# An fp32 attention + two-MoE kernel on one Trainium2 core: the second MoE's first product by seven block products instead of eight

## The chip, the cores and the metric

One core of one Trainium2 chip. The metric is device time in microseconds of one execution, the median of several runs. Engines: PE (TensorE), DVE (VectorE), ACT (ScalarE), POOL (GpSimd), SP (SyncE, which here issues most DMAs).

## What is computed

Attention with windowed masks gives x (2304 tokens x 512); a first MoE with a tanh gate gives x again; the second MoE, cut from the reference, is

```python
def _moe2_ref(x, w_in, w_out, g_ln):       # x 2304x512, w_in 512x1024, w_out 1024x512
    h = x @ w_in
    e = np.exp(h - np.max(h, axis=-1, keepdims=True))
    sm = e / (np.sum(e, axis=-1, keepdims=True) + 1e-09)
    solu = h * sm
    mu = np.mean(solu, axis=-1, keepdims=True)
    var = np.mean((solu - mu) ** 2, axis=-1, keepdims=True)
    ln = (solu - mu) / np.sqrt(var + 1e-06) * g_ln
    return ln @ w_out
```

All weights of the two MoEs are float64 at the entry.

## The kernel before

Every large product is made of three passes of float32r matmuls: each operand is split into a high part and a low part, and high x high, high x low and low x high are summed in PSUM. So one product of a 128-token tile by a 128 x 512 block of weights is three matmuls of 512 columns.

*First MoE.* Six groups of 384 tokens, 16 slices of the hidden width each; a step s does `mm1(s)` (12 matmuls into one of two banks h, L348), then `mm2(s - 5)` (12 matmuls, L375). Between them ACT and DVE make tanh (L356), the difference (L359, which frees the h bank) and its high and low parts (L362, L365). `NS` is the number of steps, 96; the last group is steps 80 to 95.

*Weights.* Each 128 x 512 block of a weight is loaded as raw int64 words (`w_load`, L90 to L95) and turned to float32 high and low parts by `w_step` (L102): ACT makes a "top" half (L111), DVE ORs it to the rest (L123), ACT makes the high part (L117), DVE the low part (L98). For the second MoE these 16 blocks are made during steps 81 to 100, one per step, into the buffers of the first MoE's `w_in`, each of which is free once the last group has used it.

*Second MoE.* 18 tiles of 128 tokens. The tokens come back from DRAM in pairs of tiles (`load_y`, L434) and are split by `split_y`: one cast on DVE (L440), one subtraction on POOL (L441), 1024 wide. Per tile: `mm3` makes h, 24 matmuls of 512 columns into two banks (L523); `softmax` (L532 to L542) takes the maximum on DVE, Exp on ACT, the product h*e on DVE, the mean and the subtraction on DVE; `fac` squares on ACT (L548) and does seven operations of one column on POOL (L549 to L555); `trz` transposes z in eight matmuls into two banks `zt` (L566) and splits it with eight pairs of 128-column instructions that also multiply by g_ln (L574, L575); `mm4` is 24 matmuls against the second weight (L585); `store` scales and writes out (L592). The loop over tiles issues `trz(i)`, `store(i-1)`, `mm3(i+2)`, `fac(i+1)`, every other time `split_y` and `load_y`, then `mm4(i)` and `softmax(i+2)`.

The order of each engine's queue is the order in which the program issues (`manual_schedule`); a queue is worked off in order, so an instruction that waits holds all behind it. Pools set which buffers are reused, and with that most waits.

Of the kernel before, what the change touches and what calls it, by code (L numbers as in the profile page):

```python
# [20 lines left out]
NTOK = B * S  # L21
# [19 lines left out]
def tile_kernel(ctx: ExitStack, tc: tile.TileContext, qk, vw, cst, w_in, w_out, w_in2, w_out2, g_ln, out):  # L41
# [5 lines left out]
    wo_p = tc.alloc_tile_pool(name="wo", bufs=1, side="left")  # L47
# [3 lines left out]
    x_p = ctx.enter_context(tc.tile_pool(name="x", bufs=2, side="right"))  # L51
# [213 lines left out]
    def pv_pe(u, pool, tag):  # L265
# [3 lines left out]
        x = xt[g, hp] = x_p.tile([128, 2, G], F32R, tag=f"x{hp}", name=f"x{g}_{hp}")  # L269
# [122 lines left out]
    def plan():  # L392
# [3 lines left out]
        for u in range(u0, u1 + 2):  # L396
# [27 lines left out]
    w2i, w2o = [None] * (2 * KD), [None] * NF2  # L424
    wq2 = [(w2i, 2 * k + n, wi_p, w_in2[k, n], f"wi{2 * k + n}", f"w2i{2 * k + n}")
           for k in range(KD) for n in range(2)]
    wq2 += [(w2o, j, wi_p, w_out2[j], f"wi{2 * KD + j}", f"w2o{j}") for j in range(NF2)]

    yt, y_raw = {}, {}

    def load_y(j):
        if j < NTOK // YT:
            y_raw[j] = p2.tile([128, KD, YT], F32, tag="yr", name=f"yr{j}")
            nc.sync.dma_start(out=y_raw[j], in_=y_dr[:, :, j * YT:(j + 1) * YT])  # L434

    def split_y(j):
        if j < NTOK // YT:
# [12 lines left out]
    for s in range(NS + LAG):  # L450
        if s == NS - NF:
            assert not todo and not later and not (wq or wld or wa or wf or wh), (todo, later)
            a_ps.release()
            at_p.release()
            qs_p.release()
            cv_p = tc.alloc_tile_pool(name="cv2", bufs=2, side="left", reuse_waits="tile")
            new_tops()
            h2a = tc.alloc_tile_pool(name="h2a", bufs=1, space=PSUM, side="right", reuse_waits="tile")
            p2 = tc.alloc_tile_pool(name="p2", bufs=2, side="right", reuse_waits="tile")
            wq.extend(wq2)  # L460
            w_load()
            w_load()
        for half in range(2):
# [8 lines left out]
            if s < NF + LAG and done[0] < W0 + WA * (slot + 1) // WB or s > NS - NF and half == 0:  # L472
                w_step()
                done[0] += 1
            follow = [fn() for fn in todo.pop(slot, [])]
# [25 lines left out]
    while wq or wld or wa or wf or wh:  # L501
        w_step()
# [12 lines left out]
    def mm3(i):  # L515
        y = yt[i // 2]
        o = (i % 2) * TT
        ps = (h2a if i % 2 == 0 else h2b).tile([128, FF2], F32, tag="h2", name=f"h2_{i}")
        for n in range(2):
            q = 0  # L520
            for k in range(KD):
                for a, b in ((0, 0), (0, 1), (1, 0)):
                    nc.tensor.matmul(ps[:, n * 512:(n + 1) * 512], y[:, a, k, o:o + TT], w2i[2 * k + n][:, b],  # L523
                                     start=(q == 0), stop=(q == 3 * KD - 1))
                    q += 1
        st[i] = dict(h=ps)

    def softmax(i):

        d = st[i]  # L530
        ps = d["h"]
        sml = p3.tile([128, 8], F32, tag="sml", name=f"sml{i}", bufs=4)  # L532
        d["sml"] = sml
        nmax, ssum, usum, nmean = (sml[:, c:c + 1] for c in range(4))
        e = p3.tile([128, FF2], F32, tag="e", name=f"e{i}")
        u = p3.tile([128, FF2], F32, tag="u", name=f"u{i}")
        d["z"], d["junk"] = e, u
        nc.vector.tensor_reduce(out=nmax, in_=ps, axis=mybir.AxisListType.X, op=ALU.max, negate=True)
        nc.scalar.activation(out=e, in_=ps, func=AF.Exp, bias=nmax, accum_out=ssum)  # L539
        nc.vector.scalar_tensor_tensor(out=u, in0=ps, scalar=1.0, in1=e, op0=ALU.mult, op1=ALU.mult, accum_out=usum)  # L540
        nc.vector.tensor_scalar(out=nmean, in0=usum, scalar1=-1.0 / FF2, scalar2=None, op0=ALU.mult)
        nc.vector.tensor_scalar(out=e, in0=u, scalar1=nmean, scalar2=None, op0=ALU.add)  # L542

    def fac(i):
# [3 lines left out]
        nc.scalar.activation(out=d["junk"], in_=d["z"], func=AF.Square, accum_out=ssq)  # L548
# [8 lines left out]
    def trz(i):  # L557

        d = st[i]
        z = p3.tile([128, 2, NF2, TT], F32R, tag="z", name=f"z{i}")  # L560
        pp = []
        for n in range(2):
            ps = zo.tile([128, 512], F32, tag="zt", name=f"zt{i}_{n}").rearrange("p (j t) -> p j t", t=TT)
            for j in range(4):
                c = 4 * n + j
                nc.tensor.transpose(ps[:, j], d["z"][:, c * TT:(c + 1) * TT], ident)  # L566
            pp.append(ps)
        for n in range(2):
            g = gl_sb[:, 4 * n:4 * n + 4].unsqueeze(2).to_broadcast([128, 4, TT])
            zh, zl = z[:, 0, 4 * n:4 * n + 4], z[:, 1, 4 * n:4 * n + 4]  # L570
            for j in range(4):
                c = 4 * n + j
                gc = gl_sb[:, c:c + 1]
                nc.scalar.activation(out=z[:, 0, c], in_=pp[n][:, j], func=AF.Copy, scale=gc)  # L574
                nc.vector.scalar_tensor_tensor(out=z[:, 1, c], in0=pp[n][:, j], scalar=gc,  # L575
                                               in1=z[:, 0, c].bitcast(F32), op0=ALU.mult, op1=ALU.subtract)
        d["zt"] = z

    def mm4(i):
        z = st[i]["zt"]  # L580
# [111 lines left out]
```

## Time and profile before

| | |
|---|---|
| runs | 729.39, 727.55, 728.31 us; median 728.31 |
| span of the profiled execution | 726.3 us |
| PE busy | 708.8 us (98%), 4160 matmuls |
| DVE, ACT, POOL busy | 440.5, 386.9, 114.4 us |
| second MoE | from 504 us to the end |

The span runs from the first to the last instruction of one profiled execution; the runs' times contain what lies around it. In the page's 40 slices PE stands at 9 tenths from the fourth slice to the last but one, with the granted clock at 9 (90% or more) throughout. `x24` means 24 instructions; `out<-in` are the program's names without buffer numbers; a duration given as a mean is that of one instruction.

### The profile page before, as it was taken

To read this page: it belongs to the slowest core of one execution; us is meant where nothing else is said; L and a number is where in the kernel's file an instruction comes from. 1 tells how busy PE (TensorE), PEld (TensorE's weight loads), DVE (VectorE), ACT (ScalarE), POOL (GpSimd) and SP (SyncE) were. 2 spreads that over 40 slices of the span, in tenths; PEclk is the share of its full clock that TensorE was granted. 3 is DMA by queue.
4 is the path that set the end of the run, shared out by engine and by line. 5 is a ranking of instruction groups with operands and counts; after the bars stand their busy time and mean duration, and the time that the engine had idled before them with its cause. 6 is when DMAs were issued, how large, how long until landed. Compare 5 with 4: busy or idle time off the path is not lost.

```text
span 726.3 us, 11583 instructions
## 1 busy us (share of the span) xinstructions
PE 708.8 (98%) x4160; PEld 650.7 (90%) x4160; DVE 440.5 (61%) x1169; ACT 386.9 (53%) x1010; POOL 114.4 (16%) x190
## 2 busy tenths in 40 slices
PE   6888999999999999999999999999999999999997
PEld 5678999999999999999999999999888888888885
DVE  5987676476676667766666435554555454555452
ACT  5778776465555555555555334543354444444444
POOL 2212311011010111111110100101133221323110
PEclk9999999999999999999999999999999999999999
DMA  9985621132223211322230015543001110110001
GB/s 274 341 263 177 189 78 55 65 110 66 66 66 109 66 60 44 107 66 66 66 109 1 1 49 170 175 142 132 1 15 59 44 58 16 59 44 30 15 29 44
DMA packets 30313, 64.05 MB, mean 88 GB/s; under 512 B 2992, under 2 KB 16816, under 8 KB 30256
## 3 DMA queue, kind: packets, MB, share of 16 engines
q1 hardware_dynamic: 27088, 58.59, 25.4%
q10 hardware_dynamic: 3168, 4.72, 1.8%
q8 instruction: 33, 0.54, 0.3%
q14 instruction: 24, 0.20, 0.1%
HBM read 53.86 MB, written 9.44 MB: 87 GB/s over the span
## 4 chain that ended last, share of the span: by engine, by line
PE 92%; DVE 4%; DMA 1%; issue 1%; ACT 1%; POOL 0%; SPq 0%; ACTq 0%; POOLq 0%
PE y L375 28%; PE h L348 26%; PE po L585 14%; PE h L523 14%; PE zt L566 2%; PE pv L275 2%; PE tp L254 2%; PE qkp L219 2%; PE qkp L199 2%; DMA qkr<-in_qk_dram 1%; DVE p L204 1%; DVE wy_wi L123 1%; DVE wi L98 1%; DVE wi L134 0%; POOL p L247 0%
## 5 line engine op out<-in xcount | busy, mean ns | idle before, releaser
L348 PE MATMUL h<-x,wi 128*128 128x384 f32 x1152 | 220.0, 340 | 1.6 <-DVE t L359 1.6
L375 PE MATMUL y<-gs,wo 128*128 128x384 f32 x1152 | 217.4, 339 | 0.0
L375 PEld LDWEIGHTS y<-gs,wo 128*128 128x128 f32 x1152 | 199.8, 189 | 1.8
L348 PEld LDWEIGHTS h<-x,wi 128*128 128x128 f32 x1152 | 197.4, 189 | 3.2 <-DVE t L359 2.1
L247 POOL TENSOR_TENSOR p<-p,rs 96x512 f32<-96x512 f32 x47 | 57.2, 1217 | 350.4 <-DVE rs L245 323.5
L365 DVE TENSOR_TENSOR gs<-t,gs 128x384 fp32r<-128x384 f32 x96 | 77.4, 806 | 52.7 <-ACT gs L362 52.6
L523 PE MATMUL h<-w2i,yt 128*128 128x512 f32 x432 | 104.9, 397 | 0.0
L585 PE MATMUL po<-w2o,z 128*128 128x512 f32 x432 | 104.1, 396 | 0.1
L574 ACT ACTIVATE z<-zt,gl_sb 128x128 fp32r<-128x128 f32 x144 | 50.9, 366 | 96.6 <-PE zt L566 48.5
L585 PEld LDWEIGHTS po<-w2o,z 128*128 128x128 f32 x432 | 80.7, 188 | 20.4 <-ACT z L574 1.9
L523 PEld LDWEIGHTS h<-w2i,yt 128*128 128x128 f32 x432 | 79.7, 187 | 18.4
L359 DVE TENSOR_TENSOR t<-h,t 128x384 f32<-128x384 f32 x96 | 53.0, 552 | 69.8 <-ACT t L356 69.7
L575 DVE SCALAR_TENSOR_TENSOR z<-zt,gl_sb,z 128x128 fp32r<-128x128 f32 x144 | 48.9, 350 | 68.9 <-ACT z L574 68.9
L356 ACT ACTIVATE t<-h 128x384 f32<-128x384 f32 x96 | 46.8, 487 | 79.4 <-PE h L348 76.4
L239 ACT ACTIVATE p<-p,nm 96x128 f32<-96x128 f32 x192 | 74.9, 392 | 21.4 <-DVE nm L204 20.8
L362 ACT CAST gs<-t 128x384 fp32r<-128x384 f32 x96 | 48.8, 508 | 46.8 <-DVE t L359 46.8
L540 DVE SCALAR_TENSOR_TENSOR u<-h,e 128x1024 f32<-128x1024 f32 x18 | 22.0, 1224 | 24.1 <-ACT e L539 24.1
L199 PE MATMUL qkp<-qkr 64*96 64x128 f32 x160 | 29.4, 339 | 7.3 <-DMA qkr<-in_qk_dram 5.4
L441 POOL TENSOR_TENSOR yt<-yr,yt 128x1024 fp32r<-128x1024 f32 x9 | 22.8, 2538 | 86.8 <-DVE yt L440 86.8
L239 ACT ACTIVATION_READ_ACCUMULATOR p<-p,nm 96x1 f32 x192 | 36.1, 188 | 0.0
L199 PEld LDWEIGHTS qkp<-qkr 64*96 64x96 f32 x160 | 24.1, 205 | 11.8 <-DMA qkr<-in_qk_dram 5.7
L286 DVE TENSOR_TENSOR x<-pv,x 128x384 fp32r<-128x384 f32 x24 | 16.3, 699 | 25.1 <-ACT x L284 24.6
(64 smaller groups left out, 657.6 us busy)
## 6 DMA issues: line engine op xcount, KB each, us to landing
qkr<-in_qk_dram SPq DMA_DIRECT2D x28, 448.0 KB, 3.4
raw_wi<-in_w_in_dram SPq DMA_DIRECT2D x16, 511.8 KB, 7.2
raw_wo<-in_w_out_dram SPq DMA_DIRECT2D x16, 511.8 KB, 6.7
v<-in_vw_dram SPq DMA_DIRECT2D x48, 128.0 KB, 3.3
y_dr<-ys ACTq DMA_DIRECT2D x6, 768.0 KB, 3.9
yr<-y_dr SPq DMA_DIRECT2D x9, 512.0 KB, 4.2
out_dram<-o SPq DMA_DIRECT2D x18, 256.0 KB, 2.0
qkr<-in_qk_dram SPq DMA_DIRECT2D x20, 224.0 KB, 4.8
```

The costliest lines, as they stand in the source:

```text
L199: nc.tensor.matmul(ps[:, b], d["r"][:64, b * NQ:(b + 1) * NQ], d["r"][:64, QC + b * NK:QC + (b + 1) * NK], start=True, stop=True)
L239: nc.scalar.activation(out=d["p"][:, b], in_=d["p"][:, b], func=AF.Exp, scale=-1.0, bias=d["nm"][:, b:b + 1], accum_out=d["sm"][:, b:b + 1])
L247: eng.tensor_tensor(out=d["p"], in0=d["p"], in1=d["rs"].unsqueeze(2).to_broadcast([NQ, 4, NK]), op=ALU.mult)
L348: nc.tensor.matmul(ps, w[:, a, k * 128:(k + 1) * 128], xt[g, k][:, b], start=(n == 0), stop=(n == 3 * KD - 1))
L359: nc.vector.tensor_tensor(out=t, in0=ps, in1=t, op=ALU.subtract)
L362: nc.scalar.copy(out=gs[:, 0], in_=t)
L365: nc.vector.tensor_tensor(out=gs[:, 1], in0=t, in1=gs[:, 0].bitcast(F32), op=ALU.subtract)
L375: nc.tensor.matmul(yb[g][m], wo[c][:, a, m * 128:(m + 1) * 128], gs[:, b], start=(c == 0 and i == 0), stop=(c == NF - 1 and i == 2))
L523: nc.tensor.matmul(ps[:, n * 512:(n + 1) * 512], y[:, a, k, o:o + TT], w2i[2 * k + n][:, b], start=(q == 0), stop=(q == 3 * KD - 1))
L574: nc.scalar.activation(out=z[:, 0, c], in_=pp[n][:, j], func=AF.Copy, scale=gc)
L575: nc.vector.scalar_tensor_tensor(out=z[:, 1, c], in0=pp[n][:, j], scalar=gc, in1=z[:, 0, c].bitcast(F32), op0=ALU.mult, op1=ALU.subtract)
L585: nc.tensor.matmul(po, z[:, a, j], w2o[j][:, b], start=(q == 0), stop=(q == 3 * NF2 - 1))
```

## The change

`mm3` now does a pair of tiles at once, and computes the product of the pair's 256 tokens by w_in2 by Strassen's method (in Winograd's form). The tokens are cut in two halves (the two tiles), the inner width of 512 in two, the output width of 1024 in two. Seven products of 6 matmuls each (`prod`) take the place of eight. They need

- on the token side, beside A11, A12, A22: S1 = A21 + A22, S2 = S1 - A11, S3 = A11 - A21 (tile `sm`) and S4 = A12 - S2 (written over A21): four POOL operations of 256 columns in `split_y`, then three casts on DVE (512, 512, 768 columns) and three subtractions on POOL for the low parts;
- on the weight side, beside B11, B21, B22: t1 to t4, eight differences on POOL (four for each half of the inner width), each split into high and low parts like a block of its own. B12 is no longer split;
- after the products, sums u2 and u3 and four results (`neg_add`, which adds, negates and takes a running minimum in one DVE instruction into SBUF). The last product, P3, is added in PSUM to P5.

Exp, h*e and the rest now read the negated h from SBUF. 256 * g_ln is the scale of the second weight's split, so z is split by two plain 512-column copies and subtractions. `w2_plan` lists by step what is done to the weights; `split_y(0)` and `split_y(1)` are issued after steps 87 and 94. In the loop over pairs the order is `split_y(i+2)`, `load_y(i+3)`, `mm4(2i+1)`, `trz(2i+3)`, `mm4(2i)`, `trz(2i+2)`, `mm3(i+2)`, and `fac` follows the softmax in `mm3`.

```diff
+    def w2_dif(kk, out, a, b):
+        fa, fb = w2f["i", kk, a], w2f["i", kk, b]
...
+        nc.gpsimd.tensor_tensor(out=o, in0=fa, in1=fb, op=ALU.subtract)
...
+    def w2_hi(key, pool, tag):
+        w = pool.tile([128, 2, 512], F32R, tag=tag, name="w2" + "_".join(map(str, key)))
+        sc = gl2[:, key[1]:key[1] + 1] if key[0] == "o" else 256.0
+        nc.scalar.activation(out=w[:, 0], in_=w2f[key], func=AF.Copy, scale=sc)
...
+    def w2_plan():
+        def do(n, fn):
+            w2s.setdefault(n, []).append(fn)
+        for kk in range(2):
+            z = 6 * kk
+            for out, a, b, n, pool, tag in (("t3", "b22", "b12", 5, wa_p, f"wo{1 + 3 * kk}"),
+                                            ("t1", "b12", "b11", 5, wi_p, f"wi{z + 1}"),
+                                            ("t2", "b22", "t1", 7, wa_p, f"wo{3 * kk}"),
+                                            ("t4", "b21", "t2", 7, wa_p, f"wo{2 + 3 * kk}")):
+                do(z + n, lambda kk=kk, out=out, a=a, b=b: w2_dif(kk, out, a, b))
+                do(z + n + 1, lambda kk=kk, out=out, pool=pool, tag=tag: w2_hi(("i", kk, out), pool, tag))
+                do(z + n + 2, lambda kk=kk, out=out: w2_lo(("i", kk, out)))
+        for i, (kind, j, nm, _) in enumerate(w2c):
+            if nm != "b12":
+                do(i + 2, lambda i=i, key=(kind, j, nm): w2_hi(key, wi_p, f"wi{i}"))
+                do(i + 3, lambda key=(kind, j, nm): w2_lo(key))
+            do(i + 1, lambda i=i: w2_or(i))
+            do(i, lambda i=i: w2_top(i))
+            do(i, lambda i=i: w2_load(i + 2))
...
     def split_y(j):
-        if j < NTOK // YT:
-            r = y_raw.pop(j)
-            y = p2.tile([128, 2, KD, YT], F32R, tag="yt", name=f"yt{j}")
-            nc.vector.tensor_copy(out=y[:, 0], in_=r)
-            nc.gpsimd.tensor_tensor(out=y[:, 1], in0=r, in1=y[:, 0].bitcast(F32), op=ALU.subtract)
-            yt[j] = y
...
+        a11, a12 = r[:, 0:2, 0:TT], r[:, 2:4, 0:TT]
+        a21, a22 = r[:, 0:2, TT:YT], r[:, 2:4, TT:YT]
+        for o, a, b, op in ((sm[:, 0], a21, a22, ALU.add), (sm[:, 1], sm[:, 0], a11, ALU.subtract),
+                            (sm[:, 2], a11, a21, ALU.subtract), (a21, a12, sm[:, 1], ALU.subtract)):
+            nc.gpsimd.tensor_tensor(out=o, in0=a, in1=b, op=op)
...
+        for sl, v in ((slice(0, 4), r[:, :, 0:TT]), (slice(4, 8), r[:, :, TT:YT]),
+                      (slice(8, 14), sm.rearrange("p s k t -> p (s k) t"))):
+            nc.vector.tensor_copy(out=yh[:, sl], in_=v)
+            nc.gpsimd.tensor_tensor(out=yl[:, sl], in0=v, in1=yh[:, sl].bitcast(F32), op=ALU.subtract)
...
+    def mm3(i, mid=()):
...
+        prod(b0, y, 0, "b11")
+        prod(b1, y, 5, "t2")
...
+        nc.scalar.copy(out=c, in_=b0)
+        nc.vector.tensor_tensor(out=u2, in0=b1, in1=c, op=ALU.add)
+        prod(b2, y, 4, "t1")
+        if 0 in mid:
+            mid[0]()
+        prod(b3, y, 6, "t3")
+        nc.vector.tensor_tensor(out=u3, in0=b3, in1=u2, op=ALU.add)
+        neg_add(i, 1, 1, b2, u3)
+        b1 = bank(sa, "b1", i, "p4")
+        prod(b1, y, 3, "t4")
+        neg_add(i, 1, 0, b1, u3)
+        if 1 in mid:
+            mid[1]()
+        softmax_e(2 * i + 1)
+        b3 = bank(sb, "b3", i, "p2")
+        prod(b3, y, 1, "b21")
+        neg_add(i, 0, 0, b3, c)
+        softmax_u(2 * i + 1)
+        prod(b2, y, 2, "b22", first=False)
+        neg_add(i, 0, 1, b2, u2)
+        softmax_e(2 * i)
+        softmax_z(2 * i + 1)
+        softmax_u(2 * i)
+        softmax_z(2 * i)
...
     mm3(0)
-    softmax(0)
-    mm3(1)
-    softmax(1)
-    fac(0)
-    for i in range(NT):
-        trz(i)
...
+    mm3(1, {0: lambda: trz(1), 1: lambda: trz(0)})
+    for i in range(NP):
+        split_y(i + 2)
+        load_y(i + 3)
+        mm4(2 * i + 1)
+        if i + 1 < NP:
+            trz(2 * i + 3)
+        mm4(2 * i)
+        if i + 1 < NP:
+            trz(2 * i + 2)
+        if i + 2 < NP:
             mm3(i + 2)
```

In the rows below, a row is line, operation, outputs <- inputs (with buffer numbers) and the output's partitions x elements.

DVE in the loop, first as it stood: the low parts of z (`z6`, L575), then the one cast of `split_y` (`yt5`), then the next tile's maximum (L538) and h*e.

```order
L575 SCALAR_TENSOR_TENSOR z6_6205<-zt6_0_6206,gl_sb_82,z6_6205 128x128 x4
L575 SCALAR_TENSOR_TENSOR z6_6205<-zt6_1_6211,gl_sb_82,z6_6205 128x128 x4
L440 CAST yt5_6268<-yr5_6074 128x1024
L538 TENSOR_REDUCE sml8_6298<-h2_8_6235 128x1
L540 SCALAR_TENSOR_TENSOR u8_6300,sml8_6298<-h2_8_6235,e8_6299 128x1024
```

And DVE in the changed loop: `hn4` is z of tile 4, `yr3` and `ysm3` the raw tokens and the sums of pair 3, `zt5` and `zt4` the PSUM banks of the transposes.

```order
L690 TENSOR_SCALAR hn4_5958<-hn4_5958,sml4_5959 128x1024
L535 CAST yt3_5992<-yr3_5816 128x512 x2
L535 CAST yt3_5992<-ysm3_5993 128x768
L717 TENSOR_TENSOR z5_6034<-zt5_0_6035,z5_6034 128x512
L717 TENSOR_TENSOR z5_6034<-zt5_1_6042,z5_6034 128x512
L717 TENSOR_TENSOR z4_6077<-zt4_0_6078,z4_6077 128x512
L717 TENSOR_TENSOR z4_6077<-zt4_1_6085,z4_6077 128x512
L651 TENSOR_TENSOR u2_3_6106<-sp6_3_6093,c_3_6110 128x512
```

The casts stood behind the low parts of z; now they stand ahead of them, and two of the three read what POOL's sums write.

POOL in the changed loop: the end of `fac` of tile 6 (L702 to L704), the four sums of pair 4 (L530), its three low parts (L536), the next `fac`.

```order
L702 TENSOR_SCALAR sml6_6147<-sml6_6147 128x1
L703 TENSOR_TENSOR sml6_6147<-sml6_6147 128x1
L704 TENSOR_TENSOR sml6_6147<-sml6_6147 128x1
L530 TENSOR_TENSOR ysm4_6181<-yr4_6004 128x256
L530 TENSOR_TENSOR ysm4_6181<-ysm4_6181,yr4_6004 128x256
L530 TENSOR_TENSOR ysm4_6181<-yr4_6004 128x256
L530 TENSOR_TENSOR yr4_6004<-yr4_6004,ysm4_6181 128x2x128
L536 TENSOR_TENSOR yt4_6180<-yr4_6004,yt4_6180 128x512 x2
L536 TENSOR_TENSOR yt4_6180<-ysm4_6181,yt4_6180 128x768
L698 MEMSET sml9_6315 128x1
```

Before, one L441 of 1024 columns stood in the place of these seven, behind the `fac` of one tile; now the `fac` of two tiles is ahead of them.

POOL in the last group of the first MoE: the differences t3 and t1 (L467), the pieces of `split_y(0)`, the differences t2 and t4 (written over `f3` and `f2`); and ACT a little later, where t2's and t4's high parts (L473) stand ahead of step 88's gs (L368) and step 89's tanh (L362).

```order
L467 TENSOR_TENSOR t3_0_5069<-f3_5029,f1_4946 128x512
L467 TENSOR_TENSOR f1_4946<-f1_4946,f0_4908 128x512
L530 TENSOR_TENSOR ysm0_5140<-yr0_5010 128x256
L530 TENSOR_TENSOR ysm0_5140<-ysm0_5140,yr0_5010 128x256
L530 TENSOR_TENSOR ysm0_5140<-yr0_5010 128x256
L530 TENSOR_TENSOR yr0_5010<-yr0_5010,ysm0_5140 128x2x128
L536 TENSOR_TENSOR yt0_5139<-yr0_5010,yt0_5139 128x512 x2
L536 TENSOR_TENSOR yt0_5139<-ysm0_5140,yt0_5139 128x768
L467 TENSOR_TENSOR f3_5029<-f3_5029,f1_4946 128x512
L467 TENSOR_TENSOR f2_4983<-f2_4983,f3_5029 128x512
```

```order
L473 ACTIVATE w2i_0_t2_5211<-f3_5029 128x512
L473 ACTIVATE w2i_0_t4_5213<-f2_4983 128x512
L473 ACTIVATE w2i_1_b11_5216<-f6_5175 128x512
L449 ACTIVATE top0_4813<-raw_w2_8_5121 128x512
L368 CAST gs88_5167<-t88_5166 128x384
L362 ACTIVATE t89_5209<-h89_5196 128x384
```

Before, POOL had only the two L441 of the first pairs in this stretch, and no high part on ACT had an input from POOL.

## Rows read from the trace of the kernel before

**Rows 1.** The page: its span, and the granted clock by slice.
```profile
span 726.3 us, 11583 instructions
...
PEclk9999999999999999999999999999999999999999
```

**Rows 2.** The chain of waits from 480 us on: start us, us, what.
```profile
489.81 2.08 PE h L348 x12
...
697.23 5.60 PE h L523 x24
702.83 5.58 PE po L585 x24
708.41 0.87 PE zt L566 x8
...
709.31 6.13 PE po L585 x24
...
716.39 6.13 PE po L585 x24
```

**Rows 3.** POOL's timeline in the loop: start us, us, engine line op out<-in count.
```profile
538.45 0.10 POOL L549 MEMSET sml<- 128x1 f32 x1
...
539.22 0.22 POOL L552 TENSOR_SCALAR sml<-sml 128x1 f32<-128x1 f32 x1
...
548.37 2.41 POOL L441 TENSOR_TENSOR yt<-yr,yt 128x1024 fp32r<-128x1024 f32 x1
...
559.23 0.21 POOL L553 TENSOR_SCALAR sml<-sml 128x1 f32<-128x1 f32 x1 [7.21 <-ACT u L548]
...
560.31 0.10 POOL L549 MEMSET sml<- 128x1 f32 x1
```

**Rows 4.** ACT's timeline at the same place.
```profile
558.01 1.06 ACT L548 ACTIVATE u<-e 128x1024 f32<-128x1024 f32 x1
...
559.62 1.12 ACT L539 ACTIVATE e<-h,sml 128x1024 f32<-128x1024 f32 x1 [0.46 <-DVE sml L538]
```

**Rows 5.** DVE's timeline at the same place.
```profile
560.85 1.22 DVE L540 SCALAR_TENSOR_TENSOR u<-h,e 128x1024 f32<-128x1024 f32 x1 [1.33 <-ACT e L539]
...
562.31 0.75 DVE L542 TENSOR_SCALAR e<-u,sml 128x1024 f32<-128x1024 f32 x1
```

**Rows 6.** POOL's timeline at two places of the first MoE.
```profile
49.53 1.91 POOL L247 TENSOR_TENSOR p<-p,rs 96x512 f32<-96x512 f32 x1 [16.87 <-DVE rs L245]
...
303.76 1.04 POOL L247 TENSOR_TENSOR p<-p,rs 96x512 f32<-96x512 f32 x1 [9.40 <-DVE rs L245]
```

**Rows 7.** DVE's timeline at the same two places.
```profile
49.85 0.68 DVE L123 SCALAR_TENSOR_TENSOR wy_wi<-raw_wi,top 128x512 int32<-128x512 int32 x1
...
303.88 1.32 DVE L365 TENSOR_TENSOR gs<-t,gs 128x384 fp32r<-128x384 f32 x1 [0.30 <-ACT gs L362]
```

**Rows 8.** DVE's groups by line and shape: busy us, mean ns of one | idle before.
```profile
L359 DVE TENSOR_TENSOR t<-h,t 128x384 f32<-128x384 f32 x96 | 53.0, 552 | 69.8 <-ACT t L356 69.7
...
L440 DVE CAST yt<-yr 128x1024 fp32r<-128x1024 f32 x9 | 6.2, 684 | 0.0
...
L98 DVE SCALAR_TENSOR_TENSOR w2o<-wy_w2o,w2o 128x512 fp32r<-128x512 f32 x8 | 5.5, 682 | 0.0
...
L134 DVE TENSOR_SCALAR wo<-wy_wo 128x512 fp32r<-128x512 f32 x2 | 0.8, 421 | 0.0
```

**Rows 9.** ACT's timeline in a step of the last group of the first MoE.
```profile
466.17 0.80 ACT L111 ACTIVATE top<-raw_w2o 128x512 f16<-128x512 bf16 x1 [2.15 <-DMA raw_w2o<-in_w_out_dram]
466.84 0.61 ACT L117 ACTIVATE w2i<-wy_w2i 128x512 fp32r<-128x512 f32 x1
...
467.75 0.48 ACT L356 ACTIVATE t<-h 128x384 f32<-128x384 f32 x1
```

**Rows 10.** Windows: us, busy us (count) of PE, PEld, DVE, ACT, POOL, PEclk, DMA, GB/s.
```profile
55.00:60.00 5.00, 2.78 (x17) 2.32 (x16) 3.94 (x16) 4.59 (x14) 1.91 (x1) 0.97 0.93 272
60.00:65.00 5.00, 5.00 (x23) 5.00 (x24) 3.95 (x9) 4.75 (x13) 1.91 (x1) 0.68 0.35 135
```

More of the change, by code (lines that the diff above doesn't have):

```diff
@@ L423, in tile_kernel @@
     NS = NG * NF
[L424 to L427, printed above, removed]
+    w2i, w2o = {}, [None] * NF2
+    gl2 = const.tile([128, NF2], F32, name="gl2")
+    w2c = []
+    for kk in range(2):
+        w2c += [("i", kk, nm, w_in2[2 * kh + kk, n]) for nm, kh, n in
+                (("b11", 0, 0), ("b12", 0, 1), ("b21", 1, 0), ("b22", 1, 1))]
+        w2c += [("o", j, "o", w_out2[j]) for j in (range(2) if kk == 0 else range(2, NF2))]
@@ L471, in tile_kernel @@
                 mm2(s - LAG)
-            if s < NF + LAG and done[0] < W0 + WA * (slot + 1) // WB or s > NS - NF and half == 0:
+            if s < NF + LAG and done[0] < W0 + WA * (slot + 1) // WB:
                 w_step()
                 done[0] += 1
+            if s > NS - NF and half == 0:
+                for fn in w2s.pop(s - (NS - NF) - 1, []):
+                    fn()
             follow = [fn() for fn in todo.pop(slot, [])]
@@ L512, in tile_kernel @@
     p3 = ctx.enter_context(tc.tile_pool(name="p3", bufs=2, side="left", reuse_waits="tile"))
     st = {}
[L515 to L526, printed above, removed]
@@ L528, in softmax, with prod @@
-    def softmax(i):
-        d = st[i]
[L531 to L540, printed above, removed]
+    def prod(ps, y, blk, w, first=True):
+        q = 0
+        for kk in range(2):
+            for a, b in ((0, 0), (0, 1), (1, 0)):
+                nc.tensor.matmul(ps, y[:, a, blk, kk], w2i[w, kk][:, b], start=first and q == 0, stop=q == 5,
+                                 skip_group_check=not first)
+                q += 1
@@ new lines, in bank, with neg_add @@
+    def bank(pool, tag, i, nm):
+        return pool.tile([128, 512], F32, tag=tag, name=f"s{nm}_{i}")
+    def neg_add(i, t, n, a, b):
+        d = st[2 * i + t]
+        if "hn" not in d:
+            d["hn"] = p3.tile([128, FF2], F32, tag="hn", name=f"hn{2 * i + t}", bufs=4)
+            d["sml"] = p3.tile([128, 8], F32, tag="sml", name=f"sml{2 * i + t}", bufs=6)
+            init, acc = 3.0e38, d["sml"][:, 7:8]
+        else:
+            init, acc = d["sml"][:, 7:8], d["sml"][:, 0:1]
+        nc.vector.tensor_tensor_reduce(out=d["hn"][:, n * 512:(n + 1) * 512], in0=a, in1=b, op0=ALU.add, op1=ALU.min,
+                                       scale=-1.0, scalar=init, accum_out=acc)
@@ new lines, in mm3 @@
+    def mm3(i, mid=()):
+        y = yt.pop(i)
+        for t in range(2):
+            st[2 * i + t] = {}
+        mid = dict(mid)
+        b0, b1 = bank(sa, "b0", i, "p1"), bank(sa, "b1", i, "p6")
+        prod(b0, y, 0, "b11")
+        prod(b1, y, 5, "t2")
+        u2 = p3.tile([128, 512], F32, tag="u2", name=f"u2_{i}", bufs=1)
+        u3 = p3.tile([128, 512], F32, tag="u3", name=f"u3_{i}", bufs=1)
+        b2, b3 = bank(sb, "b2", i, "p5"), bank(sb, "b3", i, "p7")
+        c = p3.tile([128, 512], F32, tag="c", name=f"c_{i}", bufs=1)
+        nc.scalar.copy(out=c, in_=b0)
[22 more added lines that the diff above has]
+        softmax_z(2 * i)
@@ L559, in trz @@
         d = st[i]
[L560 to L561 removed]
+        z = p3.tile([128, 2, NF2, TT], F32R, tag="z", name=f"z{i}", bufs=3)
         for n in range(2):
@@ L565, in trz @@
                 c = 4 * n + j
[L566 to L569, printed above, removed]
+                nc.tensor.transpose(ps[:, j], d["hn"][:, c * TT:(c + 1) * TT], ident)
             zh, zl = z[:, 0, 4 * n:4 * n + 4], z[:, 1, 4 * n:4 * n + 4]
[L571 to L576, printed above, removed]
+            nc.scalar.copy(out=zh, in_=ps)
+            nc.vector.tensor_tensor(out=zl, in0=ps, in1=zh.bitcast(F32), op=ALU.subtract)
         d["zt"] = z
     def mm4(i):
-        z = st[i]["zt"]
+        d = st.pop(i)
+        z = d["zt"]
         po = zo.tile([128, DM], F32, tag="po", name=f"po{i}")
```

121 lines of the change are left out of this document (84 added, 37 removed).

## The prediction

> **What bounds the kernel now.** I read the page first: the span and the granted clock [rows 1]. TensorE (PE) runs at the upper of its two levels (2.4 GHz) over the whole span. Then the chain of waits [rows 2]: over the last 220 us, the second MoE, it is PE end to end, a repeating 5.60 us (24 matmuls of the first product, `mm3`), 5.58 us (24 of the second, `mm4`) and 0.87 us (8 transposes, `trz`). No engine makes PE wait there until the last two tiles, where `mm4` takes 6.13 us because z arrives in 128-wide parts. So PE work that goes is time that goes, as long as nothing else becomes late. The rest of the reading is about that: what POOL, ACT and DVE take for one piece of work [rows 3 to 5], what they take from each other [rows 6, 7], and shapes near the new ones [rows 8].
>
> Two things must be seen in these rows. POOL is slow for its size: 1024 elements per partition take 2.41 us [rows 3], 512 take 1.04 us [rows 6], and the seven one-column operations of `fac` take 0.99 us (first four) and 1.08 us (last three) [rows 3]. And POOL and DVE shut each other out, when DVE reads two operands from SBUF: L365 began 0.12 us behind POOL's L247 and took 1.32 us, where the like shape of L359 takes 0.55 [rows 8], ending 0.4 us after POOL; the other way round POOL's L247 at 49.53 took 1.91 us, and got its turn only when DVE's L123 ended at 50.53 [rows 6, 7].
>
> **The change, part by part.** *Seven products for eight.* Per pair of tiles `mm3` issues 42 matmuls of 512 columns in place of 48: 54 fewer in nine pairs. One costs 5.60 / 24 = 0.233 us [rows 2]: **-12.6 us**, all on the path.
>
> *The tail.* The last two `mm4` no longer follow their own transposes at once (`mm4` of tile 17 stands between), and z comes in 512-wide parts: 2 x (6.13 - 5.58) = **-1.1 us** [rows 2]. The last store stays.
>
> *Wider z parts, g_ln in the weights.* 144 + 144 instructions of 128 columns become 36 + 36 of 512 on ACT and DVE. Neither engine bounds the loop before; by itself 0, hidden under `mm4`.
>
> *The loop over pairs.* Time zero is PE's hand-over from the last product of a pair (P3) to `mm4`. After it PE has 5.58 + 0.87 + 5.58 us of ready work, so the second `trz` is due at 12.03. It needs the first PSUM bank `zt`, which DVE frees with the low part of z of the tile before (L717 of the changed kernel). In DVE's order that instruction stands behind the three casts of `split_y`, and the second cast waits for POOL's four sums, which stand behind both tiles' `fac`. Step by step, 0.1 us per hand-over between engines:
> - P4 ends at -2.8; its minimum (0.68 for 512 columns with one PSUM operand, on the line from 0.55 for 384 to 1.22 for 1024 [rows 5, 8], and 0.08 for the accumulator) to -1.9; Exp 1.23 to its user's start [rows 4, 5]; DVE's product u of 1024, 1.3, until 0.7.
> - The last minimum, 0.7 to 1.45. Exp to 2.8. Product, mean and subtraction: 560.85 to 562.31, then 0.75 [rows 5], until 5.0. Square, 1.22 to POOL's start [rows 3, 4]: 6.3.
> - POOL is later than that. Of the first tile's last three operations one fits at 4.05; then DVE's subtraction and first cast hold it off until 5.35. Two more to 6.2, four for the second tile to 7.1, three to 8.2.
> - Four sums of 256. No row has this shape: on the line from 0.22 (one column) to 1.04 (512) [rows 3, 6] one is 0.63. With two waits inside, 2.6: until 10.8. Bounds: 0.52 (half of 1.04) and 0.77 (the line to 2.41 for 1024). I take 0.63, since L247 has the same output type and the nearest size.
> - POOL goes on with its first low part (512, 1.31 on the line to 2.41) before DVE has heard of the sums, and shuts the casts out: 12.1. Cast two ends 0.3 later, cast three (768; 0.55 between 0.42 and 0.68 [rows 8]) at 12.85, the low part of z at 13.5.
> - PE gets the bank at 13.6, 1.55 late; the second bank costs 0.15 more. **1.7 us per pair.** The third low part of `split_y`, wanted by the third matmul of the second product, is done before PE asks.
>
> Seven pairs have a `split_y` ahead of them in the loop: 7 x 1.7 = **+11.9 us**. Ends: 0.6 per pair (sums at 0.52, POOL never held off) and 2.7 (0.77, and every low part meeting a DVE operation): 4.2 to 18.9.
>
> By the Trainium skill (GPSIMD Engine Reference, section on performance versus the Vector engine), an fp32 tensor_tensor of 2048 takes 4497 ns on this engine, twice DVE's time; a sum of 256 would be 0.56 us, an estimate from that page. The stall would be 1.4 us and the total 2 us lower. The trace's 2.41 us for 1024 is 7% above that rate.
>
> *The weights, under the last group of the first MoE.* A step there is two pieces of 2.08 us on PE [rows 2]. There are 22 high and low parts in place of 16, and eight differences on POOL. In seven of the steps nothing is late: ACT waits 2.15 us for a load in a step as it is [rows 9]. But `split_y(0)` comes between the differences: its three low parts are ahead of t2 and t4 in POOL's queue. From the start of slot 88: DVE's casts, low parts and ORs keep POOL off until 3.45 (six operations of 0.4 to 0.68 [rows 8]); low parts until 4.65, 7.0 (held once more) and 8.7, differences until 9.75 and 10.85. ACT stands at the high part of t2 and t4, and behind these come another high part, a top half whose load has landed by then, gs and tanh (0.61, 0.80 and twice 0.48, less what neighbours overlap [rows 9]): tanh ends at 13.5, DVE frees the h bank at 14.2. PE wants it at 3 x 4.16 = 12.5: **+1.7 us**, once; 0.8 to 3 by how often POOL is held off. SP is held too: the second load of y waits for POOL and two weight loads stand behind it; they land in time.
>
> *The first two pairs.* In the second `mm3` ACT's copy of P1 is behind the second Square of pair 0, which ends at 6.3; copy 0.6, sum u2 0.7. P4 needs the bank that u2 frees at 7.7 and is due at 4.2 + 0.87 + 1.4 = 6.5: **+1.2 us**, once; 0.8 to 1.8.
>
> Sum: -12.6 - 1.1 + 11.9 + 1.7 + 1.2 = +1.1 us: a span of 727.4 us. The median of the runs, 728.3, is 2.0 above the span of 726.3 [rows 1]; so **729.4 us**. 0.3%, about what a measurement of this kernel can tell from no change, is 2.2 us: the forecast is no change, because the stall in the loop eats what the products save.
>
> **The rivals.**
> *The stall is a third of that* (0.6 us): POOL's sums take 0.52 us and its small operations are not held off. For it: the lines through POOL's rows rest on few points, and a one-column operation may slip between two DVE instructions. Against it: L247 had to wait through two DVE instructions in a row [rows 6, 7]. 4.2 for 11.9: -6.6, 721.7 us. Slope: 0.1 us of a sum is 2.8 us of the kernel.
> *POOL is slower than my line* (2.2 to 2.7 us per pair): a piece of 256 goes at the rate of L441, whose shape (two full operands) is the sums' own, while L247 reads one operand broadcast. It decides from 0.67 us for a sum on (0.16 us more stall per pair): then the kernel is slower by over 0.3%. At 0.77: 7 x 2.2 = 15.4, +4.6; at the end of the bounds +8.1: 733 to 736 us, 734 the likeliest.
> *No stall in the loop*: DVE gets past the casts in time. It would need the sums 1.6 us sooner, against all rows read; -10.8, 717.5 us.
> *The clock falls behind the gaps.* In 60 to 65 us the granted clock averaged 0.68, that is partly the lower level (1.2 GHz), after 5 us in which PE was busy for 2.78 [rows 10]. A fall like it costs 5 x 0.32 = 1.6 us; seven of them 11 us, 740 us. Against it: here PE is idle for 1.7 of 24 us. By the Trainium skill (TensorE: Matmul & The Clock Gate, section on why this matters for your kernels), idle gaps between bursts of matmuls lower the clock; by that rule a gap that is long enough would do this. The trace has one such fall, and gaps in the stretch before it.
>
> **How the numbers follow.** Forecast 0.37, third of the stall 0.23, slower POOL 0.32, no stall 0.05, clock 0.03. The forecast's own spread (the one-time stalls, 0.2 us per pair) is mostly inside 2.2 us: 0.32 of it is no change, 0.02 faster, 0.03 slower; the edges of the two POOL cases add 0.03 to no change. Faster: 0.22 + 0.05 + 0.02 = 0.29. Same: 0.35. Slower: 0.30 + 0.03 + 0.03 = 0.36. The range reaches to the two POOL cases: 722 to 735 us; the forecast alone has 727.4 to 731.5.
>
> **What would show it.** PE's waits should name DVE's L717 ahead of `zt`, twice for each of seven pairs, 1.7 us per pair; the three casts in DVE's timeline should stand 5 us apart between the first and the second; POOL's L530 should take 0.6 to 0.65 us. One gap of 1 to 2 us should lie near 474 us, before an `h` matmul, and one in the second pair before P4. A product should still take 1.40 us. The prediction is wrong if L717 is not waited for, or if L530 takes 0.5 or 0.8 us.

## The result, and the profile after

| | before | changed |
|---|---|---|
| runs on one chip | 4, median 728.38 us | 4, 733.12 to 735.53, median 733.79 us |
| ratio | | 1.0076, interval 1.0057 to 1.0095 |
| span of the profiled execution | 726.3 us | 733.7 us (of a run of 735.53) |
| matmuls | 4160 | 4106 |

The change makes the kernel slower by 0.76%, 5.4 us. The page and PE's waits, to read beside [rows 1]. The profiled run is the slowest of the four. A line of the waits is: engine, tile and line that waits, `<-` engine, tile and line waited for: us in total, times, longest. Of the tiles, `h` is a bank of the first MoE's `mm1`, `zt` of the transposes, `sp` of the seven products and `po` of `mm4`; the seven are issued as P1, P6, P5, P7, P4, P2, P3.

```profile
span 733.7 us, 11467 instructions
...
PEclk9999999999999999999999999899999999999999
```

```profile
PE zt L714 <- DVE z L717: 10.2, 7, 1.6
...
PE h L354 <- DVE t L365: 4.3, 2, 3.0
...
PE sp L618 <- DVE u L651: 0.9, 1, 0.9
```

Three new waits, at the three places that the prediction named: seven before `zt`, one before an `h` (of the two, the shorter, 1.3 us, is also in the kernel before), one before P4. And one slice of the granted clock at 8, which is new.

The chain of waits in the loop, to read beside [rows 2]. Before, it was PE alone; now it goes through POOL's sums and DVE's casts in every pair.

```profile
568.28 1.44 POOL ysm L530 x2
570.57 1.97 DVE yt L535 x2
573.20 1.25 PE zt L714 x8
574.45 5.61 PE sp L618 x24
...
597.55 1.26 PE zt L714 x8
...
696.27 9.80 PE sp L618 x42
706.07 5.50 PE po L727 x24
...
718.82 11.03 PE po L727 x48
```

A pair now takes 597.55 - 573.20 = 24.35 us. Two `mm4` of 5.50, two `trz` of 0.87 and a product part of 9.80 would be 22.54. So the stall is 1.8 us per pair: the wait, 1.4 us (1.6 the first time), and a `zt` group of 1.25 in place of 0.87. The products themselves did what they should: 42 matmuls in 9.80 us, 0.233 us each as before. The `mm4` take 5.50 in place of 5.58, and the last two together 11.03 in place of twice 6.13.

DVE's timeline and then POOL's, at the same pair (start us, us, engine, line and operation, and in brackets the idle time before and who ended it; POOL answers to [rows 3]):

```profile
564.83 0.42 DVE L535 CAST yt<-yr 128x512 fp32r<-128x512 f32 x1
570.57 1.50 DVE L535 CAST yt<-yr 128x512 fp32r<-128x512 f32 x1 [5.33 <-POOL yr L530]
571.99 0.55 DVE L535 CAST yt<-ysm 128x768 fp32r<-128x768 f32 x1
572.46 1.28 DVE L717 TENSOR_TENSOR z<-zt,z 128x512 fp32r<-128x512 f32 x2
```

```profile
566.92 0.58 POOL L704 TENSOR_TENSOR sml<-sml 128x1 f32<-128x1 f32 x1
567.46 0.74 POOL L530 TENSOR_TENSOR ysm<-yr 128x256 f32<-128x256 f32 x1
...
569.80 0.74 POOL L530 TENSOR_TENSOR yr<-yr,ysm 128x256 f32<-128x256 f32 x1
570.50 1.29 POOL L536 TENSOR_TENSOR yt<-yr,yt 128x512 fp32r<-128x512 f32 x1
```

This is the predicted order of events: DVE stands 5.33 us at the second cast, until the fourth sum ends at 570.54; POOL starts its first low part before DVE has heard of it, and the second cast, 0.42 us alone, takes 1.50 and ends 0.3 behind POOL; two more DVE operations, and PE gets its bank.

The other place is the last group of the first MoE: DVE's timeline, the start of step 88 on PE, POOL's timeline, the chain, and windows (us, busy us and count of PE, granted clock, DMA share, GB/s).

```profile
464.40 1.78 DVE L479 SCALAR_TENSOR_TENSOR w2i_t<-t,w2i_t 128x512 fp32r<-128x512 f32 x1
466.10 1.78 DVE L479 SCALAR_TENSOR_TENSOR w2i_t<-f,w2i_t 128x512 fp32r<-128x512 f32 x1
467.80 2.33 DVE L479 SCALAR_TENSOR_TENSOR w2o_o<-f,gl,w2o_o 128x512 fp32r<-128x512 f32 x1
470.06 1.76 DVE L457 SCALAR_TENSOR_TENSOR f<-raw_w,top 128x512 int32<-128x512 int32 x1
471.74 1.61 DVE L371 TENSOR_TENSOR gs<-t,gs 128x384 fp32r<-128x384 f32 x1
...
475.67 0.55 DVE L365 TENSOR_TENSOR t<-h,t 128x384 f32<-128x384 f32 x1
```

```profile
462.44 2.24 PE L354 MATMUL h<-x,wi 128*128 128x384 f32 x12
```

```profile
467.29 2.29 POOL L536 TENSOR_TENSOR yt<-ysm,yt 128x768 fp32r<-128x768 f32 x1
469.55 3.39 POOL L467 TENSOR_TENSOR f<-f,f 128x512 f32<-128x512 f32 x2
```

```profile
473.36 0.48 DVE t L365
...
473.88 4.21 PE h L354 x12
478.09 2.91 PE y L381 x12
481.00 2.12 PE h L354 x12
```

```profile
470.00:474.00 4.00, 1.04 (x7) 0.86 0.59 208
474.00:478.00 4.00, 4.00 (x13) 0.50 0.00 0
478.00:482.00 4.00, 4.00 (x20) 0.78 0.40 135
```

Two things happen. Five DVE operations that take 0.55 to 0.74 us alone take 1.61 to 2.33 each: POOL works through `split_y(0)` and two differences meanwhile, and the two engines hold each other up. PE waits 2.96 us, at the `h` group of step 90. Then the granted clock is 0.50 for the next 4 us (all at the lower level, 1.2 GHz), and two groups of 2.08 us take 4.21 and 2.91: another 3.0 us.

### The profile page after: what moved, and what is told of

Read it like the earlier page. It is cut to its first block, busy times and chain, and to the rows that moved or that the text cites. A ratio compares the mean times of both kernels' runs of the same rounds, so it can differ in the third digit from the quotient of the medians.

```text
span 733.7 us, 11467 instructions
## 1 busy us (share of the span) xinstructions
PE 702.3 (96%) x4106; PEld 645.5 (88%) x4106; DVE 459.3 (63%) x1157; ACT 367.7 (50%) x917; POOL 185.6 (25%) x253
## 5 line engine op out<-in xcount | busy, mean ns | idle before, releaser
L354 PE MATMUL h<-x,wi 128*128 128x384 f32 x1152 | 223.7, 343 | 4.4 <-DVE t L365 4.3
L727 PE MATMUL po<-w2o_o,z 128*128 128x512 f32 x432 | 102.6, 394 | 0.0
L365 DVE TENSOR_TENSOR t<-h,t 128x384 f32<-128x384 f32 x96 | 53.0, 552 | 70.6 <-ACT t L362 70.6
L727 PEld LDWEIGHTS po<-w2o_o,z 128*128 128x128 f32 x432 | 80.5, 188 | 17.3
L362 ACT ACTIVATE t<-h 128x384 f32<-128x384 f32 x96 | 46.8, 488 | 82.8 <-PE h L354 79.7
L368 ACT CAST gs<-t 128x384 fp32r<-128x384 f32 x96 | 48.6, 507 | 46.7 <-DVE t L365 46.6
L678 ACT ACTIVATE e<-hn,sml 128x1024 f32<-128x1024 f32 x18 | 20.8, 1153 | 67.1 <-DVE sml L634 50.5
L618 PE MATMUL sp<-w2i_t,yt 128*128 128x512 f32 x216 | 52.4, 396 | 0.9 <-DVE u L651 0.9
L618 PEld LDWEIGHTS sp<-w2i_t,yt 128*128 128x128 f32 x216 | 40.4, 188 | 11.0 <-DVE u L651 1.4
L618 PE MATMUL sp<-w2i_b,yt 128*128 128x512 f32 x162 | 41.2, 399 | 0.0
L535 DVE CAST yt<-yr 128x512 fp32r<-128x512 f32 x18 | 15.0, 843 | 37.3 <-POOL yr L530 37.3
L618 PEld LDWEIGHTS sp<-w2i_b,yt 128*128 128x128 f32 x162 | 29.8, 188 | 6.5
L205 PEld LDWEIGHTS qkp<-qkr 64*96 64x96 f32 x160 | 24.1, 205 | 11.9 <-DMA qkr<-in_qk_dram 5.8
L730 ACT ACTIVATE o<-po,sml 128x512 f32<-128x512 f32 x18 | 12.2, 679 | 42.8 <-POOL yt L536 25.0
```

What stands on the lines that cost most here:

```text
L205: nc.tensor.matmul(ps[:, b], d["r"][:64, b * NQ:(b + 1) * NQ], d["r"][:64, QC + b * NK:QC + (b + 1) * NK], start=True, stop=True)
L354: nc.tensor.matmul(ps, w[:, a, k * 128:(k + 1) * 128], xt[g, k][:, b], start=(n == 0), stop=(n == 3 * KD - 1))
L362: nc.scalar.activation(out=t, in_=ps, func=AF.Tanh)
L365: nc.vector.tensor_tensor(out=t, in0=ps, in1=t, op=ALU.subtract)
L368: nc.scalar.copy(out=gs[:, 0], in_=t)
L618: nc.tensor.matmul(ps, y[:, a, blk, kk], w2i[w, kk][:, b], start=first and q == 0, stop=q == 5, skip_group_check=not first)
```

## The experiments

Each ratio is to the kernel before on the same chip; the changed kernel stands at 1.0076. A hundredth of a per cent is 0.07 us.

### POOL's sums ahead of the softmax's small operations

In the loop the two `fac` are issued behind the split of the next pair instead of inside the softmax. Their Squares keep their place on ACT; only POOL's order changes.

```diff
     def softmax_z(i):
...
-        fac(i)
...
+    fac(1)
+    fac(0)
     for i in range(NP):
         split_y(i + 2)
         load_y(i + 3)
+        if i + 1 < NP:
+            fac(2 * i + 3)
+            fac(2 * i + 2)
```

> One move against the changed kernel: on POOL the next pair's sums of y are issued ahead of the one-column operations (fac) of the softmax of z instead of behind them; the orders on ACT and DVE stay as they are. Theory (the casts wait for sums that stand behind fac on POOL, which itself waits for DVE and ACT): the sums run while TensorE is at mm3, the casts are done before the low parts of z, the seven waits of zt of 1.5 us go, and with them some 0.2 us each in the group's own time: 721 to 724. Rival 1 (POOL and DVE hold each other's operands up, so that POOL's 10 us of each pair decide): half of the waits stay, 727 to 730. Rival 2 (the sums, earlier, hold up DVE's work for the softmax of z, so zt waits for ACT or DVE as long as before): 732 to 735.

Measured: 720.31 us against 727.13, ratio 0.9896 (0.9880 to 0.9912): 1.80% or 13.1 us below the changed kernel. Of its waits on PE from 380 us on, two are left; its chain in the loop is PE alone again.

```profile
PE h L354 <- DVE t L365: 2.5, 1, 2.5
PE sp L618 <- DVE u L651: 0.9, 1, 0.9
```

```profile
548.46 0.87 PE zt L713 x8
549.33 9.79 PE sp L618 x42
...
571.00 0.87 PE zt L713 x8
```

The theory holds, with a time a little below the one expected, and both rivals fall: a pair takes 22.54 us, nothing of the stall is left, though POOL has the same work and the two engines still hold each other up (the third cast takes 1.64 us, for 0.55 in the changed kernel). By the two profiles the stall was 10.2 us of waits and 7 x 0.38 of longer `zt` groups, 12.8 us; by the times it is 13.1.

### The split behind the transposes

```diff
-        split_y(i + 2)
-        load_y(i + 3)
         mm4(2 * i + 1)
         if i + 1 < NP:
             trz(2 * i + 3)
+        split_y(i + 2)
+        load_y(i + 3)
         mm4(2 * i)
```

> One move against the changed kernel: the split of the next pair's y (POOL's sums and low parts, DVE's casts) is issued behind the transposes of z of the next tile instead of ahead of them, so DVE's low parts of z stand ahead of the casts on its queue. Theory (the seven waits of 1.5 us before zt are DVE's low part of z queued behind a cast that waits for POOL's sums and low parts): no wait of zt on z of more than 0.2 us is left; instead the casts come after the low parts and the third of them is late for the pair's first products by up to 1 us per pair; time 726 to 729 (733.8 less 7 x 1.6, plus 7 x 0.5 to 1). Rival (POOL's own work of about 10 us per pair sets the pace whatever the order of the queues): the wait only moves from zt to sp, 733 to 735.

Measured: 730.36 us, ratio 1.0047 (1.0026 to 1.0068), 2.1 us below the changed kernel. No wait before `zt`, but one in each of the seven pairs before the third matmul of the second product (P6), of 1.2 us where I expected up to 1:

```profile
PE sp L618 <- POOL sml L698: 8.5, 7, 1.4
```

(The releaser's name is that of the POOL operation behind the last low part.) The time lies between the two expectations. The first half of the theory holds, the wait before `zt` is the place of the casts; but with the casts put last, the last of POOL's low parts comes too late, since the sums still stand behind `fac`.

### One more sum

In each of the seven splits in the loop the first sum is made twice, in a kernel without the shift of tiles that is told of below (alone 1.0040).

```diff
+        if j >= 2:
+            nc.gpsimd.tensor_tensor(out=sm[:, 0], in0=a21, in1=a22, op=ALU.add)
```

> The changed kernel without the shift of tiles, and with one more sum of 256 columns (0.74 us in the trace, its result written over with the same values) on POOL in each of the seven splits in the loop. Theory (the casts, and with them the low parts of z and PE, wait for the end of the chain of sums): each wait before zt grows by 0.7 to 0.8 us, 7 x 0.75 = 5.2 us on top of the kernel without the shift: ratio to the kernel before 1.010 to 1.012. Rival (PE waits because DVE and POOL share their port, not because of the chain's length): the wait grows by less than 0.3 us each, ratio 1.004 to 1.007.

Measured: 743.83 us, ratio 1.0219 (1.0203 to 1.0236): 13 us for seven operations of 0.74 us, far outside both. Waits, the 24 matmuls behind the first gap in the chain, and windows at the next four of the seven gaps:

```profile
PE zt L716 <- DVE z L719: 15.4, 7, 2.4
```

```profile
546.17 6.85 PE sp L620 x24
```

```profile
569.00:575.00 6.00, 3.77 (x16) 0.80 0.26 46
595.00:601.00 6.00, 3.89 (x21) 1.00 0.12 18
621.00:627.00 6.00, 3.89 (x15) 0.74 0.28 57
647.00:653.00 6.00, 3.78 (x17) 0.85 0.17 26
```

The waits grew from 9.5 us (in the kernel without the shift) to 15.4, 0.84 each: the first half is as the theory said, the chain of sums sets the wait one to one. The rest is the clock. Behind five of the seven gaps, now 2.1 to 2.4 us, it fell: in four of them the next 24 matmuls took 6.8 to 7.2 us for 5.61, behind the last gap 42 took 10.9 for 9.8. With the longer `zt` groups behind three of the gaps that is 7.8 us. In the changed kernel no gap of 1.4 to 1.6 us was followed by a fall.

### The first pair's casts and low parts a step later

```diff
+        yt[j] = (r, y, sm)
+
+    def cast_y(j):
...
+        if s == NS - NF + 8:
+            cast_y(0)
```

`split_y` is now the sums alone; `cast_y` makes the high and low parts, for the first pair one step later, elsewhere right behind. The sums of the first pair stay where they were (they start at 459.31 us, for 459.27 in the changed kernel): what moves is the casts and low parts, behind the differences t2 and t4 in POOL's queue. The load of the second pair's tokens goes with them.

> One move against the changed kernel, in the first pair only: POOL's sums of y of the first pair are issued at the end of step 87, the low parts and the casts at the end of step 88, instead of all at step 88. Theory (the new wait of 2.96 us at 470.9 us, before h, is the chain of differences of the second weights on POOL and DVE that the split of the first pair's y holds up; the granted clock falls behind that gap): the wait is under 1 us, the granted clock stays at 1 from 474 to 481 us, and the two together give 4 to 5 us of a profile in which the clock fell and 3 to 4 us of the median: 729 to 731. Rival (the weights' own work on POOL and DVE is too much for its steps, wherever the split stands): a wait of 2 to 3 us stays, at the same step or the one before, 733 to 735.

Measured: 730.02 us, ratio 1.0037 (1.0025 to 1.0049), 2.8 us below the changed kernel, a little less than the 3 to 4 I expected. The wait at this place, and the window behind it:

```profile
PE h L354 <- DVE t L365: 0.6, 1, 0.6
```

```profile
474.00:478.00 4.00, 3.40 (x19) 1.00 0.73 257
```

The theory holds: of the wait 0.6 us is left, and the fall is gone. That the median gains less than the profiles (2.4 us of wait and 3 of clock) fits the fall not coming in every run. The four runs of the changed kernel have mean granted clocks of 0.992 (the profiled one) to 0.998; and in the profiles of four other runs that keep this gap at 2.5 to 3.0 us (the sums ahead, the split behind the transposes, and the two kernels without the shift of tiles, with and without one more sum), the first two show the fall, at 1.5 us each, and the other two have a granted clock of 1.00 behind it.

### g_ln and the wide z parts alone

The kernel before, with these two parts of the change and eight products.

> The kernel before with only the two small parts of the change: g_ln multiplied into the second weight matrix, and the parts of z in passes of 512 columns; the products stay eight blocks. Theory: the passes save the tail's 1.1 us and nothing else is on the path: 726.5 to 727.8 against 728.4. Rival (wider passes make TensorE wait longer for the first low part of z in every tile): 728.5 to 732.

Measured: 729.09 us, ratio 1.0032 (1.0020 to 1.0044), slower by 2.3 us. The theory's saving did not come; the rival's time did, but not its mechanism, since there is no new wait. The last tile's `mm4` still stands behind its own transposes and takes 6.1 us, so the width alone does not give the tail's gain. What is left is the order of the pairs, which was not run alone. But PE, never idle there, lost 2 us over the first MoE, long before most of what this edit touches runs. What differs up there is one thing: the tile `gl2` of 32 bytes, which moves all weights' tiles 32 bytes further.

### The place of the tiles

The kernel before with one unread tile of 32 bytes (`pad`), and the changed kernel with g_ln scaled in its own tile (`gl2 = gl_sb`), so that nothing is moved.

```diff
+    pad = const.tile([128, NF2], F32, name="pad")
+    nc.gpsimd.memset(pad, 0)
```

> The kernel before with one more tile of 32 bytes behind g_ln's that nothing reads (zeroed once on POOL); nothing else differs. Theory (the place of the weights' tiles): slower by 1.5 to 2 us, with a median of 337 ns at h and y: 728.7 to 729.2 against 727.1. Rival: no change, 726.9 to 727.4.

> The changed kernel with g_ln scaled in its own tile, so that no second tile of 32 bytes stands ahead of the weights: every tile behind it lies where it lay before the change. In the profiles with the second tile the 1152 matmuls of 384 columns at h and the 1152 at y have a median of 337 ns instead of 336, and PE reaches 430 us about 2 us later with no idle time of its own. Theory (the place of the weights' tiles, 32 bytes further on, costs each of these matmuls 0.7 to 0.9 ns): the median is 336 ns again, the second MoE starts 1.5 to 2 us earlier, 1.5 to 2 us off the time: 730.5 to 731.5 against 732.5 of the change on this chip. Rival (run to run, or the code's own size and order): no change, 732 to 734.

Measured: with the tile 1.0024 (1.0010 to 1.0037), 1.7 us slower; the changed kernel without its own 1.0040 (1.0026 to 1.0053), 2.6 us below the change. Both theories hold, the second by 0.6 us more than it said; its profile also lacks the fall of the clock in the first MoE. Then the question of a rule:

> The kernel before with an unread tile of 64 bytes, instead of 32, behind g_ln's. With 32 bytes the median matmul of 384 columns took 337 ns for 336 and the kernel 1.8 us longer. Theory (what counts is where the weights' tiles stand modulo 64 bytes): the time of the kernel before, 336 ns, within 0.5 us. Rival (each step away from the old place costs, or the distance to the tiles on the other side does): 1.8 us or more, 337 ns.

> The same with an unread tile of 96 bytes. Theory (modulo 64 bytes): as with 32 bytes, 1.8 us over the kernel before, 337 ns. Rival (only the first 32 bytes, or the distance): not 1.8 us: either no loss or a larger one.

Measured: 64 bytes 1.0014 (0.9998 to 1.0030), 96 bytes 1.0011 (0.9997 to 1.0025): neither can be told from no change, nor, by the times alone, from 32 bytes. The timelines of PE show more than the totals: the same two groups of `mm1` in the kernel before, with 32 bytes and with 64.

```profile
126.15 2.33 PE L348 MATMUL h<-x,wi 128*128 128x384 f32 x12
...
460.52 2.24 PE L348 MATMUL h<-x,wi 128*128 128x384 f32 x12
```

```profile
126.66 2.33 PE L350 MATMUL h<-x,wi 128*128 128x384 f32 x12
...
462.54 2.24 PE L350 MATMUL h<-x,wi 128*128 128x384 f32 x12
```

```profile
125.11 2.35 PE L350 MATMUL h<-x,wi 128*128 128x384 f32 x12
...
462.64 2.24 PE L350 MATMUL h<-x,wi 128*128 128x384 f32 x12
```

The same work takes 334.4, 335.9 and 337.5 us (and 335.1 with 96 bytes), PE busy throughout. The theory of 64 bytes falls here: 64 should have been like no shift, and took longest. Chance from run to run is not the cause: over the same two groups the three other profiles without the shift all have 334.5 us, and the six others with 32 bytes 335.9 or 336.1. With 64 bytes the second MoE gives 1.8 us back: its product takes 5.46 to 5.51 us for 5.60. So the place of tiles is worth up to 3 us in a stage, of either sign. No rule came out, and the median time of a matmul, by which I had judged, is no guide: it was 334 ns with 64 bytes, where the first MoE took longest.

### Together

The sums first, the first pair's casts a step later, and in the second `mm3` `fac(1)` and `fac(0)` behind `trz(1)`, so that ACT's copy of P1 comes ahead of their Squares:

> The changed kernel with three moves: POOL's sums of y ahead of the softmax's one-column operations in every pair, the sums of the first pair a step ahead of their casts, and the two one-column operations of the first pair behind the transposes of the last tile, so that fewer waits stand before the second pair's fourth product. Theory (the parts are independent, each at its own place on the path): 12 us for the first by its own run, 2.6 for the second, 0.5 to 0.9 for the third off 732.5: 716.5 to 718. Rival (the first pair's sums, a step earlier, and the sums of the second pair collide in the passage between the weights and the loop, so that a part of the second's gain goes): 718 to 720.

Measured: 715.30 us, ratio 0.9835 (0.9815 to 0.9856). The theory holds, by a little more than it said; the wait before P4 is gone.

The same three with g_ln scaled in its own tile, so without the shift of tiles:

> The kernel of the three moves with g_ln scaled in its own tile, so that the weights' tiles lie where they lay before the change. Theory: 1.5 to 2 us below the kernel of the three moves, 714.5 to 716.5. Rival (the place of the tiles costs nothing): the same as the three moves.

Measured: 712.89 us against 728.06, ratio 0.9800 (0.9786 to 0.9813), 2.4 us below the one before it where 1.5 to 2 were expected. This version beats the kernel before by 15 us. Its chain is PE to the end:

```profile
538.34 9.80 PE sp L627 x42
548.14 5.49 PE po L735 x24
```

## Why the prediction was right and wrong

The range (722 to 735) held the time, but the likeliest case, no change at 729.4, did not come: it is slower by 0.76%. The stall in the loop came as foretold; two other terms of the sum were off, the last group of the first MoE with the clock behind it, and the place of the tiles. The sum was +1.1 us against 7.4 between the two profiled spans and 5.4 between the medians. Term by term, by the profiles:

| term | forecast | measured |
|---|---|---|
| 54 matmuls | -12.6 | -12.6 |
| tail | -1.1 | -1.2 |
| the other `mm4` | 0 | 16 x 0.08 = -1.3 |
| stall in the loop | +11.9 | 10.2 + 7 x 0.38 = +12.8 |
| last group of the first MoE | +1.7 | +3.0 wait, +3.0 clock |
| P4 in the second pair | +1.2 | +0.9 |
| place of the tiles | 0 | +1.9 |

The seven make +6.5 of 7.4; about 0.6 more is the first MoE's remaining groups, 2.12 us instead of 2.08. The fall is not the cause of these: the kernel with the casts a step later has 2.12 us there too, without a fall. The remaining 0.3 us I cannot place.

*The loop was right in its mechanism and nearly in its size, by errors that cancel.* I took 0.63 us for a sum, from the line through L247's 512 columns; it takes 0.74, near my upper bound of 0.77, which came from L441, whose two full operands are the sums' own shape. Four sums ended 3.0 us after `fac` where I had 2.6. But `fac` ended at 567.50, 7.6 us after PE's hand-over, where I had 8.2: I had POOL's small operations held off more than they were. PE asked for its bank 0.16 us sooner, its `mm4` being shorter, and the second bank cost 0.38 us where I had 0.15; it shows in the length of the `zt` group, so that L717 is waited for once per pair and not twice. The estimate of 0.56 us per sum, worked out from the Trainium skill (GPSIMD Engine Reference, section on performance versus the Vector engine), is further off than either line; the measured 0.74 decides. By the point I gave (0.67 us), the rival of a slower POOL is the case that came, and its 733 to 736 us holds the time; but its stall of 2.2 us per pair did not come, and most of what lay above the forecast was elsewhere. That its likeliest time, 734 us, was nearly met is luck.

*The last group of the first MoE was mis-sized: +1.7 us for a measured 6.0.* The path that I priced was near. Counted from the start of step 88 (462.44), POOL's low parts ended at 7.1 us where I had 8.7, its differences, at 472.94, at 10.5 where I had 10.85, and the `h` bank behind ACT's tanh came free at 13.8 where I had 14.2. But PE had been stopped one step sooner, and there the path was not ACT but DVE. The step that failed is the time of DVE's operations: I let the casts, low parts and ORs take their time alone, 3.45 us for six of them, and only POOL be held off. DVE worked without a gap, but at 1.6 to 2.3 us for operations that take 0.55 to 0.74 alone, so the instruction that frees the bank for step 90 (L365) ran only at 473.3. I had counted what DVE costs POOL, one delay at a time, and not what POOL costs DVE in return when both have a full queue. By the Trainium skill (SBUF — State Buffer, section on the two separate sides) the two share a port pair, for which a DVE operation with two inputs from SBUF contends with a POOL operation that reads SBUF: whoever starts first holds it for its whole instruction, while the other blocks. The trace agrees, with 1.78 us for DVE's low parts, where 0.68 is the time alone.

*The clock was a rival in the wrong place.* I gave it 0.03 and only for the loop's gaps. There it did not come; it came behind the one longer gap, which I had priced at its length alone: 3.0 us that the sum had at nothing. The run with one more sum shows how near the loop was: 0.8 us more per gap, and the rival's picture came, with some 8 of its 11 us.

*What could not be in the sum:* the 32 bytes of `gl2`, 1.9 us in the profile. The trace of before shows no row of it.

*Left open:* why `mm4` gains 0.08 us each (not from the wide z, whose run alone has 5.57, nor from the 32 bytes, without which the last version has 5.49; the place of the second weight's own tiles could do it, as 64 bytes did to the first product, but that wasn't tried); and what about an address makes PE slower.

## What to carry to other kernels

When an engine's queue gets a block of work that others wait for, ask what stands ahead of it that waits itself: here four sums whose inputs had long been there stood behind fourteen one-column operations that waited for two other engines, and turning the two round was worth 13 us, the whole difference between a loss and a gain. Price a gap on PE at more than its length, and two full queues on DVE and POOL at more than the sum of their parts. And when an edit changes the size of a tile, compare a stage that the edit does not touch: it can have moved by 2 us.

## What the runs showed of the hardware that I had not expected

- Gaps of 1.4 to 1.6 us in the loop left the granted clock at 1.00; of gaps of 2.1 to 2.4 us, five of seven were followed by a fall that cost 1.1 to 1.6 us in the next product; of single gaps of 2.5 to 3.0 us in the first MoE (five profiles), three were, for 1.5 to 3.0 us, and two were not; the lengths of both kinds overlap.
- Moving all weights' tiles by 32, 64 or 96 bytes changed a stretch of 334 us of matmuls by +1.5, +3.2 and +0.7 us, with PE never idle; kernels with the same place agree to 0.2 us.
- A POOL sum of 256 columns with two operands takes 0.74 us alone, and 0.81 to 1.19 in the last group of the first MoE, where DVE is busy.
